# A convolution, routing and expert kernel with its first 32 row tiles in six groups instead of five, a first chunk of 12 tiles, and ranks formed by 0/1 products

## The chip, the cores and the metric

One core of a Trainium2 chip. The metric is device time in microseconds (us) of one execution of the whole program; lower is better. The engines are named PE (matrix products; PEld is its weight load), DVE (vector), ACT (scalar activation), POOL (GpSimd) and SP (which issues most DMAs).

## What is computed

x has 8 sequences of 3584 rows with 192 values. Each of 8 heads (24 columns) gets its own causal convolution of 7 taps, whose taps are a softmax of `weight`. The 28672 resulting rows go through a routed feed-forward layer with 8 experts, where each row goes to its best expert alone.

```python
w = exp(weight - max); w /= sum(w) + 1e-9          # 8 heads x 7 taps
y[b, s, head] = sum_k w[head, k] * x_pad[b, s + k, head]
logits = y @ w_gate + modality_bias[modality_id]   # 28672 x 8
e = argmax(logits); gate = softmax(logits)[e]
out = gate * (relu(y @ w1[e]) @ w2[e])             # 192 -> 1024 -> 192
```

## The kernel before

**Tiles, groups, chunks.** A tile is 120 rows of one sequence; 4 tiles are a quad, and `QUADS_OF_GROUP` cuts the 240 tiles into 18 groups. For each group (class `Group`) the kernel loads x (`load`, L284), convolves it head by head as a product with a band matrix made from the taps (`convolve`, L304: PE into PSUM, ACT or DVE copies it to `y`), turns each quad by a DVE transpose (`turn`, L344), multiplies by the gate weights (`gate`, L362), turns the product back and adds the modality bias (`logits`, L372), picks the expert (`choose`, L382), and ranks the rows (`place`, L416). The rank of a row is its expert's base plus the number of earlier rows of that expert. `send` (L445) then scatters each tile's rows by an indirect DMA on POOL into the DRAM buffer `routed_rows`, sorted by expert. Several groups form a chunk (`GROUPS_OF_CHUNK`).

**Slots.** When a chunk is ranked, `table` (L556) finds which experts have enough rows for a full slot. A slot of the first chunk is 512 rows of one expert, a slot of the second 1024; the first two chunks have two slots each. A slot (class `Slot`) loads the expert's weights (L678 to L683) and its rows (`bring`, L689), splits both in a high and a low part on ACT and DVE (L102, L104), and runs steps: `first` (L775) multiplies rows by 128 columns of w1 (five products of 512 columns, L784), ACT and DVE make the activated `hh` and `hl` (L787, L788), and `second` (L791), two steps later, multiplies those by w2 (L802, L806). `put` and `store` write the result.

**Order.** In the head, `start` (L977) runs the groups of the first chunk to the end, loads the first slot's rows, then runs the groups of the second chunk. From there `run` (L923) goes through the steps and, by the table `marks` of due times, lets the remaining groups advance a piece at a time between steps; `prepare` adds one piece of the next chunk's table per step. Within an engine the program is one fixed order; engines wait for each other by semaphores. On each engine a waiting instruction holds back everything behind it.

**What the change touches in the head.** `WARM` (L26) is the number of products without use that run while the first inputs arrive. The gate weights are laid out in `make_gate` (L175), the band in `make_bands` (L142), the modality ids in `make_modality` (L196), all before the first group. Early groups (`whole_x`, `whole_y`) are convolved and gated in full fp32. Their x tiles share two buffers, `xh` and `xl` (L269), so a later group's x waits until an earlier group is convolved.

```python
w1b = [const.tile([P, 4, FF], F32R, name="w1b0")]                       # L94
self.x = xp.tile([P, NT, D], F32, name="x", tag=self.place_x)           # L269
ins = nc.scalar.dma_start(out=scr[DUMMY:DUMMY + TW, :]...               # L645
```

Of the kernel before, what the change touches and what calls it, by code (L numbers as in the profile page):

```python
# [28 lines left out]
AHEAD = 0  # L29
UNIT = 256  # L30
LONG = 512
GROUPS_OF_CHUNK = (3, 2, 2, 2, 2, 2, 2, 2, 1, 0, 0)
# [9 lines left out]
def conv_then_routed_ffn(ctx, tc, x, weight, modality, w_gate, mod_bias, w1, w2, out):  # L42
# [21 lines left out]
    assert NG == sum(GROUPS_OF_CHUNK) and sum(QUADS_OF_GROUP) == 2 * NSB and NB == 8 and DB == 64 and CAP < 32768 and N % TW == 0  # L64
# [29 lines left out]
    w1b = [const.tile([P, 4, FF], F32R, name="w1b0")]  # L94
    w2b = [const.tile([P, NF, 2 * D], F32R, name="w2b0")]
# [35 lines left out]
    for n in {4 * q for q in QUADS_OF_GROUP}:  # L131
        keep[n] = const.tile([MB, E, n], F32, name=f"keep{n}")
        nc.vector.memset(keep[n], 1.0)
        nc.vector.memset(keep[n][:, :, 0:1], 0.0)
# [5 lines left out]
                   base=0, channel_multiplier=0, allow_small_or_imprecise_dtypes=True)  # L140

    def make_bands():  # L142
# [20 lines left out]
        with tc.issue_after(lined):  # L163
            clear_y()
# [3 lines left out]
        for h in range(0, H, H // 2):  # L168
            nc.sync.dma_start(out=band[:, h:h + H // 2, :], in_=bass.AP(lines.tensor, h * wide, [[1, P], [wide, H // 2], [1, MB]]))
        hi = const.tile([P, H, MB], F32R, name="band_hi")  # L170
        lo = const.tile([P, H, MB], F32R, name="band_lo")
        split(hi, lo, band)
        return band, hi, lo

    def make_gate():  # L175

# [5 lines left out]
        wgs = w1b[0].rearrange("p c n -> p (c n)")[:, 0:NK * 2 * E].rearrange("p (k e) -> p k e", k=NK)  # L182
        nc.scalar.copy(out=wgs[:, :, 0:E], in_=wg)
        nc.vector.tensor_tensor(out=wgs[:, :, E:2 * E], in0=wg, in1=f(wgs[:, :, 0:E]), op=ALU.subtract)
        whole = const.tile([P, NK, P], F32, name="wg_whole", tag="w2b1")
        with tc.issue_after(state["lined"]):
            nc.gpsimd.memset(whole, 0.0)
        parts = const.tile([P, NK, P], F32R, name="wg_parts")
        nc.vector.tensor_copy(out=parts, in_=whole)
        for q in range(P // Q):  # L190
            rows = slice(q * Q, (q + 1) * Q)
            nc.vector.tensor_copy(out=whole[rows, :, q * Q:q * Q + E], in_=wg[rows])
            nc.vector.tensor_copy(out=parts[rows, :, q * Q:q * Q + 2 * E], in_=f(wgs[rows]))
        return whole, parts

    def make_modality():  # L196
# [7 lines left out]
        for half, raw in enumerate(raw2):  # L204
            spare = raw.rearrange("p c d -> p (c d)")
            ids = spare[:, P:P + some * 2 * MB].bitcast(I32).rearrange("p (b u) -> p b u", b=some)
            for i, n in ((0, NSB - 2), (NSB - 2, 2)):
                nc.scalar.dma_start(out=ids[i:i + n],
                                    in_=bass.AP(modality.bitcast(I32).tensor, 2 * (half * some * S + starts[i]),
                                                [[2 * (starts[i + 1] - starts[i]), n], [2 * S, some], [1, 2 * MB]]))  # L210
            low = xp.tile([NSB, some, MB], F32, name="low", tag=f"xr_{half + 1}", bufs=1)
            nc.vector.tensor_copy(out=low, in_=ids[0:NSB].rearrange("p b (s two) -> p b s two", two=2)[:, :, ::-1, 0])
            for b in range(some):
                nc.tensor.transpose(out=mt_ps[:, (half * some + b) * NSB:(half * some + b + 1) * NSB],
                                    in_=low[:, b, :], identity=ident[0:NSB, 0:NSB])
# [16 lines left out]
    def clear_y():  # L232
        for y in y_order:
            nc.gpsimd.memset(y[MB // Q * Q:P], 0.0)
# [12 lines left out]
    def pace(ins):  # L247
        if "result" in state:
            tc.add_manual_dep(ins, state["result"].name,
                              mybir.DependencyInfo(mybir.DependencyClass.Sync, mybir.DependencyReason.DATA), reason="pace")  # L250
# [10 lines left out]
    class Group:  # L261


        def __init__(self, g, chunk):
            self.chunk, self.xr, self.whole_x, self.whole_y = chunk, [], g < WHOLE_X, g < WHOLE_Y
            self.first = g < WHOLE_X
            self.place_x = ("xh", "xl")[g % 2 if self.whole_x else 0]
            if self.whole_x:
                self.x = xp.tile([P, NT, D], F32, name="x", tag=self.place_x)  # L269
            self.quads, before = QUADS_OF_GROUP[g], sum(QUADS_OF_GROUP[:g])  # L270
# [760 lines left out]
```

## Time and profile before

| | us |
|---|---|
| median of 3 runs (1272.39 to 1274.27) | 1272.42 |
| the profiled execution, its own time | 1272.72 |
| its span | 1271.0 |
| PE busy in the span | 1216.2 |
| DVE, ACT, POOL busy | 953.3, 687.3, 538.9 |

The profile page gives busy time per engine over the whole span; it is an average over stages. The span is read in two parts: a head, up to the first product of the first slot (61.10 us, line L784), and the long run of steps behind it. A table of busy time by stretch tells which engine fills a stretch and at which clock PE ran (1.00 is the upper of its two levels, 0.50 the lower). The chain of waits is followed back from the last instruction: it names what was waited for last, in order of time.

### The profile page before, as it was taken

Reading aid. Unit: us, or ns where it says so; the run is one execution under the profiler, and the core shown is the slowest. Engines: PE = TensorE matmul, PEld = TensorE weight load, DVE = VectorE, ACT = ScalarE, POOL = GpSimd, SP = SyncE. Lnnn points to the kernel's source line nnn. Section 1 sums busy time; section 2 is a strip of 40 time slices with the busy share of each in tenths; the row PEclk is TensorE's granted clock in tenths of the full one; section 3 lists DMA queues with packets and bytes.
Section 4 is the critical chain, followed back from the end, with each engine's and each line's share of the span. In section 5 each row is a group of like instructions: output and inputs, shape, how many; then the busy total and the mean of one; then the engine's idle time right before and its main releaser. Section 6 shows DMA issues by size and latency. Waiting matters only on the chain.

```text
span 1271.0 us, 23085 instructions
## 1 busy us (share of the span) xinstructions
PE 1216.2 (96%) x6950; PEld 1085.3 (85%) x6950; DVE 953.3 (75%) x2233; ACT 687.3 (54%) x1486; POOL 538.9 (42%) x549
## 2 busy tenths in 40 slices
PE   8589999999999999999999999999999999999995
PEld 6567777888889898989989888888988888888995
DVE  5767786778788877888778877777775666677894
ACT  3256545555556555555656555555544544555783
POOL 5723673535454534445454634525334322112222
PEclk9899999999999999999999999999999999999998
DMA  5858454442545265522545343524225433696441
GB/s 148 252 138 200 116 166 98 96 121 57 145 96 160 59 145 122 134 47 59 142 95 138 81 113 65 123 57 116 54 58 115 107 58 97 138 248 160 128 110 29
DMA packets 309872, 145.90 MB, mean 115 GB/s; under 512 B 222775, under 2 KB 296160, under 8 KB 309737
## 3 DMA queue, kind: packets, MB, share of 16 engines
q1 hardware_dynamic: 284994, 98.97, 36.2%
q0 software_dynamic: 22464, 44.31, 11.4%
q10 hardware_dynamic: 2279, 1.06, 0.3%
q8 instruction: 56, 0.92, 0.3%
q14 instruction: 79, 0.65, 0.2%
HBM read 114.84 MB, written 51.82 MB: 131 GB/s over the span
## 4 chain that ended last, share of the span: by engine, by line
PE 69%; DVE 12%; issue 6%; DMA 5%; ACT 3%; POOL 3%; SPq 0%; DVEq 0%; POOLq 0%; ACTq 0%
PE hps L784 32%; PE po L802 20%; PE po L806 9%; PE cv L314 4%; PE gt L368 3%; DVE hl L788 2%; POOL out_dram L824 1%; DVE turned L348 1%; DMA routed_rows<-y,idx 1%; DVE sxs L770 1%; DMA raw<-in_moe_w_dram 1%; DVE w1b L104 1%; DVE gx L104 1%; DVE tp L742 1%; DMA rows<-routed_rows 1%
## 5 line engine op out<-in xcount | busy, mean ns | idle before, releaser
L802 PE MATMUL po<-w2b,hh 128*128 128x384 f32 x1824 | 556.9, 359 | 5.5 <-DVE o L820 4.7
L806 PE MATMUL po<-w2b,hl 128*128 128x192 f32 x1824 | 458.9, 252 | 0.0
L787 ACT ACTIVATE hh<-hps 128x512 fp32r<-128x512 f32 x456 | 272.2, 598 | 344.3 <-PE hps L784 330.6
L788 DVE SCALAR_TENSOR_TENSOR hl<-hps,hh 128x512 fp32r<-128x512 f32 x456 | 310.6, 684 | 192.1 <-ACT hh L787 189.3
L824 POOL DMA_INDIRECT out_dram<-o,tags x228 | 244.2, 1071 | 374.3 <-DVE o L820 208.9
L784 PE MATMUL hps<-sxh,w1b 128*128 128x512 f32 (+1 forms) x976 | 385.7, 398 | 9.0 <-DVE hl L788 8.5
L241 POOL DMA_INDIRECT routed_rows<-y,idx x220 | 240.9, 1095 | 318.6 <-DVE hl L788 134.4
L802 PEld LDWEIGHTS po<-w2b,hh 128*128 128x128 f32 x1824 | 343.0, 188 | 31.5 <-DVE o L820 9.6
L806 PEld LDWEIGHTS po<-w2b,hl 128*128 128x128 f32 x1824 | 347.8, 191 | 18.4
L784 PE MATMUL hps<-sxs,w1b 128*128 128x512 f32 (+1 forms) x976 | 291.9, 380 | 0.0
L784 PEld LDWEIGHTS hps<-sxh,w1b 128*128 128x128 f32 x976 | 184.3, 189 | 36.8 <-DVE hl L788 13.8
L784 PEld LDWEIGHTS hps<-sxs,w1b 128*128 128x128 f32 x976 | 179.4, 188 | 38.2
L784 PE MATMUL hps<-sxl,w1b 128*128 128x512 f32 (+1 forms) x488 | 185.6, 380 | 0.0
L104 DVE TENSOR_TENSOR w1b<-raw,w1b 128x512 fp32r<-128x512 f32 x148 | 99.9, 685 | 18.4 <-ACT w1b L102 16.7
L818 ACT ACTIVATE lowp<-po,tags 128x192 f32<-128x192 f32 x228 | 83.8, 420 | 38.0 <-DVE o L820 31.9
L784 PEld LDWEIGHTS hps<-sxl,w1b 128*128 128x128 f32 x488 | 93.2, 191 | 3.6 <-DVE sxl L770 0.2
L102 ACT CAST w1b<-raw 128x512 fp32r<-128x512 f32 x148 | 89.6, 618 | 10.0 <-DMA raw<-in_moe_w_dram 9.3
L820 DVE SCALAR_TENSOR_TENSOR o<-po,tags,lowp 128x192 f32<-128x192 f32 x228 | 83.8, 408 | 14.0 <-ACT lowp L818 13.8
L319 ACT COPY y<-cv 120x192 f32<-120x192 f32 (+1 forms) x192 | 51.7, 320 | 73.7 <-PE cv L314 66.4
L104 DVE TENSOR_TENSOR w2b<-raw,w2b 128x384 fp32r<-128x384 f32 x148 | 79.7, 548 | 14.8 <-ACT w2b L102 14.8
L102 ACT CAST w2b<-raw 128x384 fp32r<-128x384 f32 x148 | 73.7, 511 | 0.7
L768 ACT CAST sxh<-tp 128x512 fp32r<-128x512 f32 (+1 forms) x60 | 35.7, 596 | 49.5 <-DVE tp L742 48.8
(161 smaller groups left out, 975.0 us busy)
## 6 DMA issues: line engine op xcount, KB each, us to landing
raw<-in_moe_w_dram SPq DMA_DIRECT2D x37, 768.0 KB
raw<-in_moe_w_dram SPq DMA_DIRECT2D x37, 512.0 KB
raw<-in_moe_w_dram SPq DMA_DIRECT2D x74, 256.0 KB
rows<-routed_rows SPq DMA_DIRECT2D x208, 64.0 KB
xr<-in_x_dram SPq DMA_DIRECT2D x32, 384.0 KB
x<-in_x_dram SPq DMA_DIRECT2D x26, 384.0 KB
ends<-routed_rows SPq DMA_DIRECT2D x208, 32.0 KB
routed_rows<-filler SPq DMA_DIRECT2D x8, 776.0 KB
```

Source lines behind the costliest of these rows:

```text
L102: nc.scalar.copy(out=hi, in_=raw)
L104: return nc.vector.tensor_tensor(out=lo, in0=raw, in1=f(hi), op=ALU.subtract).ins
L241: state["scatter"] = nc.gpsimd.indirect_dma_start(out=scr, out_offset=bass.IndirectOffsetOnAxis(ap=idx, axis=0), in_=src, in_offset=None,).ins
L319: nc.scalar.copy(out=y[0:MB, 0:self.nb, ys], in_=src)
L784: nc.tensor.matmul(hps[:, u, :], wa[:, c, fs], mv[z], start=n == 0, stop=n == len(terms) - 1)
L787: nc.scalar.activation(out=hh, in_=hps, func=AF.Relu)
L788: state["result"] = nc.vector.scalar_tensor_tensor(out=hl, in0=hps, scalar=0.0, in1=f(hh), op0=ALU.max, op1=ALU.subtract).ins
L802: nc.tensor.matmul(po, hh[:, u, js], wb[:, c, :], start=c == 0, stop=c == NF - 1, skip_group_check=True)
L806: nc.tensor.matmul(po[:, 0:D], hl[:, u, js], wb[:, c, 0:D], start=False, stop=False, skip_group_check=True)
L818: nc.scalar.activation(out=lowp, in_=po[:, D:2 * D], func=AF.Copy, scale=gate)
L820: nc.vector.scalar_tensor_tensor(out=o, in0=po[:, 0:D], scalar=gate, in1=lowp, op0=ALU.mult, op1=ALU.add)
L824: st = nc.gpsimd.indirect_dma_start(out=out, out_offset=bass.IndirectOffsetOnAxis(ap=tag.bitcast(I32)[:, j, 1:2], axis=0), in_=o, in_offse ...
```

## The change

- The first eight quads form six groups (1, 1, 1, 1, 2, 2 quads) instead of five (1, 1, 2, 2, 2). The first chunk has three groups, which are now 12 tiles (16 before); the second has three groups, 20 tiles (16 before). The other groups and all slots stay as they are.
- x of groups 2 to 5 gets buffers of its own (`x_first`, `x_next`) in the space of the first split weights; the loads are issued behind the band's load and wait for no earlier group.
- For these groups the rank is formed in PSUM alone: 0/1 products add the expert's base, all earlier tiles, and the earlier rows of the tile (`place_early`). The scan, the copies of counts and one addition on DVE go.
- The first 8 heads are convolved ahead of the modality ids, the gate layout, the tables and the filler. The gate weights are cleared by DVE and laid out by ACT. What only later groups need (the band's and the gate's split parts) is made just before the first slot (`make_late`). The rows of filler are written behind the first exponential.
- `choose` makes the one-hot choice ahead of the exponential.
- Group 6 (four quads, the first that is not in full fp32 gating) is convolved at the end of the head; `parts_of` counts its heads no longer. The last group of the head is chosen and placed behind that.
- `WARM` falls from 50 to 34.

```diff
-QUADS_OF_GROUP = (1, 1, 2, 2, 2) + (4,) * 13
-WHOLE_X = 10
-WHOLE_Y = 5
+QUADS_OF_GROUP = (1, 1, 1, 1, 2, 2) + (4,) * 13
+WHOLE_X = 11
+WHOLE_Y = 6
-WARM = 50
+WARM = 34
-GROUPS_OF_CHUNK = (3, 2, 2, 2, 2, 2, 2, 2, 1, 0, 0)
+GROUPS_OF_CHUNK = (3, 3, 2, 2, 2, 2, 2, 2, 1, 0, 0)
...
-    w1b = [const.tile([P, 4, FF], F32R, name="w1b0")]
-    w2b = [const.tile([P, NF, 2 * D], F32R, name="w2b0")]
+    x_first = const.tile([P, 16, D], F32, name="x_first", tag="w1b0")
+    x_next = const.tile([P, 8, D], F32, name="x_next", tag="w2b0")
+    w1b, w2b = [], []
...
+    def fill_gate():
         for q in range(P // Q):
             rows = slice(q * Q, (q + 1) * Q)
+            with tc.issue_after(state["ids"]):
+                nc.scalar.copy(out=wg_whole[rows, :, q * Q:q * Q + E], in_=wg[rows])
+
+    def make_late():
...
+        split(hi, lo, band)
...
+        split(wgs[:, :, 0:E], wgs[:, :, E:2 * E], wg)
...
+        nc.scalar.copy(out=parts.rearrange("p k (h n) -> p (k h) n", h=2), in_=filler[:, 2:2 + P // 2].unsqueeze(1).broadcast_to([P, 2 * NK, P // 2]))
...
             else:
-                nc.sync.dma_start(out=xr, in_=x[b0:b0 + 4, starts[sb] - HALO:starts[sb] + MB, :].rearrange("b s d -> s b d"))
+                with tc.issue_after(state["band" if self.g <= WHOLE_Y else "load"]):
+                    nc.sync.dma_start(out=xr, in_=x[b0:b0 + 4, starts[sb] - HALO:starts[sb] + MB, :].rearrange("b s d -> s b d"))
...
+        def place_early(self, after):
+
+            n = self.tiles
+            oh = self.oh
+            rp = self.bank("place", [MB, n + 1, E], F32, "rp")
+            terms = [(rp[:, 0:n, :], tri, oh), (rp[:, n, :], ones, oh[:, n - 1, :]), (rp[:, 1:n, :], ones, oh[:, 0:n - 1, :])]
+            terms += [(rp[:, t:n + 1, :], ones, oh[:, 0:n + 1 - t, :]) for t in range(2, n + 1)]
+            row = tri[0:1, 0:1].broadcast_to([1, E])
+            if self.chunk == 0:
+                terms = [(rp, ones, head_oh[:, t, :].unsqueeze(1).broadcast_to([MB, n + 1, E])) for t in range(self.before)] + terms
+                row = starts_of
+            terms = [(rp, ones[0:1, :], row.unsqueeze(1).broadcast_to([1, n + 1, E])), *terms]
+            for i, (dst, wt, mv) in enumerate(terms):
+                state["ranked", self.g] = nc.tensor.matmul(dst, wt, mv, start=i == 0, stop=i == len(terms) - 1).ins
...
+            if after.g == WHOLE_Y:
+                for h in range(H):
+                    after.convolve(h)
+                    yield
+                state["ready"] = True
+                yield
+            cur.choose()
...
-        through("groups", 1)
...
+        while "ready" not in state:
+            advance()
+        with tc.issue_after(state["exp"]), tc.issue_after(state["placing"]):
+            state["late"] = make_late()
...
         with tc.issue_after(state["placing"]):
             made[i].turn(0)
-        while state["parts"] < head + AHEAD:
-            with tc.issue_after(state["vector"]):
+        with tc.issue_after(state["vector"]):
+            while state["groups"] < FIRST:
                 advance()
```

**PE ahead of the first slot's rows.** `cv` is a convolution, `gt` the gate product, `rp` the rank product, and the `po` rows are the transposes of the first slot's rows; before:

```order
L368 MATMUL gt<-turned,wg_whole 128x128 x9
L314 MATMUL cv<-x,band 120x384 x2
L422 LDWEIGHTS tri
L422 MATMUL rp<-oh,tri 120x64
L423 LDWEIGHTS ones
L423 MATMUL rp<-oh,ones 120x64
L751 MATMUL po<-raw_1_88,raw_1_86 128x128 x4
```

and with the change:

```order
L390 MATMUL gt<-turned,wg_whole 128x128 x4
L336 MATMUL cv<-x,band 120x384
L390 MATMUL gt<-turned,wg_whole 128x128 x6
L336 MATMUL cv<-x,band 120x384 x7
L826 MATMUL po<-raw_1_88,raw_1_86 128x128 x4
```

All eight heads of the first four-quad group (two before) now stand ahead of the transposes.

**POOL's first scatters.** `y...` is the source of a group's scatters; an IOTA ahead of them writes the row numbers; before:

```order
L412 IOTA raw_1_86 120x4
L241 DMA routed_rows<-raw_1_86,idx 238592x194 x4
L412 IOTA y_218 120x4
L241 DMA routed_rows<-y_218,idx 238592x194 x4
L412 IOTA y_219 120x8
L241 DMA routed_rows<-y_219,idx 238592x194 x8
```

and with the change:

```order
L252 DMA routed_rows<-raw_1_86,idx 238592x194 x4
L438 IOTA y_183 120x4
L252 DMA routed_rows<-y_183,idx 238592x194 x4
L438 IOTA y_184 120x4
L252 DMA routed_rows<-y_184,idx 238592x194 x4
```

The first chunk ends with the 12th scatter instead of the 16th.

**DVE between the first two steps of the first slot.** `hl` is a step's second half; with the change:

```order
L422 TENSOR_REDUCE first<-rk 120x8
L433 TENSOR_REDUCE den<-ex 120x8
L423 TENSOR_TENSOR oh<-rk,first 120x64
L434 TENSOR_SCALAR den<-den 120x8
L104 TENSOR_TENSOR w2b_852<-raw_0_87,w2b_852 128x2x192
L436 RECIPROCAL y_185<-den 120x8
L485 TENSOR_TENSOR pos<-rp,carry 120x64
L487 TENSOR_TENSOR carry<-rp,carry 120x8
L486 TENSOR_TENSOR pos<-pos,oh 120x64
```

Before, only the four passes on `w2b` stood there; the last head group's choice and rank now stand among them.

## Rows read from the trace of the kernel before

**Rows 1.** The page: span, and PE's busy time, share and instructions.

```profile
span 1271.0 us, 23085 instructions
PE 1216.2 (96%) x6950; PEld 1085.3 (85%) x6950; DVE 953.3 (75%) x2233; ACT 687.3 (54%) x1486; POOL 538.9 (42%) x549
```

**Rows 2.** Busy time by stretch: stretch, its length, engines, PE clock, DMA share, GB/s.

```profile
50.00:60.00 10.00, 0.86 (x5) 0.78 (x6) 4.08 (x11) 2.28 (x4) 7.85 (x9) 0.68 0.76 202
80.00:90.00 10.00, 8.79 (x49) 7.55 (x48) 9.91 (x24) 7.30 (x15) 0.00 (x0) 1.00 0.00 0
...
200.00:1200.00 1000.00, 990.57 (x5618) 890.55 (x5617) 757.59 (x1680) 553.38 (x1164) 416.24 (x412) 1.00 0.46 107
```

**Rows 3.** The chain of waits, its first 100 us: start, length, what.

```profile
16.97 8.53 DMA x<-in_x_dram
...
50.50 4.83 DMA routed_rows<-y,idx
55.53 3.67 DMA raw<-routed_rows
...
90.32 4.84 DMA raw<-in_moe_w_dram
```

**Rows 4.** Timeline, ACT: start, length, instruction, idle time before it and releaser.

```profile
12.34 0.99 ACT L102 CAST band_hi<-band 128x960 fp32r<-128x960 f32 x1 [4.35 <-DMA band<-tap_lines]
```

**Rows 5.** Timeline, PE's products; a head or gate of fp32 is two instructions.

```profile
14.57 3.60 PE L314 MATMUL cv<-x,band 128*120 128x96 f32 x32
...
20.14 2.94 PE L368 MATMUL gt<-turned,wg_whole 128*128 128x128 f32 x24 [1.97 <-DVE turned L348]
...
34.50 2.11 PE L314 MATMUL cv<-x,band 128*120 128x192 f32 x12
...
59.33 1.09 PE L751 MATMUL po<-raw,raw 128*128 128x128 f32 x4 [9.14 <-DMA raw<-routed_rows]
...
61.10 1.22 PE L784 MATMUL hps<-sxh,w1b 128*128 128x512 f32 x2
...
75.05 1.47 PE L314 MATMUL cv<-x,band 128*120 128x384 f32 x4
```

**Rows 6.** Timeline, PE: the two rank products of one group.

```profile
36.77 0.24 PE L422 MATMUL rp<-oh,tri 120*120 120x64 bf16 x1 [0.16 <-DVE oh L401]
...
36.85 0.22 PE L423 MATMUL rp<-oh,ones 120*120 120x64 bf16 x1
```

**Rows 7.** Timeline, DVE: first and last pass of one choice, and one turn.

```profile
34.70 0.32 DVE L375 STREAM_TRANSPOSE lt<-gt 128x128 f32<-128x128 f32 x1 [0.50 <-PE gt L368]
...
36.51 0.21 DVE L401 TENSOR_TENSOR oh<-rk,first 120x64 bf16<-120x64 f32 x1
...
37.84 0.96 DVE L348 STREAM_TRANSPOSE turned<-y_early 128x768 f32<-128x768 f32 x1
```

**Rows 8.** Timeline, POOL: the first scatter, and two that follow each other.

```profile
30.01 1.18 POOL L241 DMA_INDIRECT routed_rows<-raw,idx  x1 [9.71 <-ACT y L319]
...
32.80 0.99 POOL L241 DMA_INDIRECT routed_rows<-raw,idx  x1 [0.30 <-issue]
34.10 0.99 POOL L241 DMA_INDIRECT routed_rows<-raw,idx  x1 [0.30 <-issue]
```

**Rows 9.** Busy time by stretch around two pauses of PE, columns as in rows 2.

```profile
24.00:25.00 1.00, 0.00 (x0) 0.00 (x0) 0.17 (x2) 0.00 (x0) 0.00 (x0) 1.00 0.64 192
...
27.00:28.00 1.00, 1.00 (x5) 1.00 (x5) 0.91 (x6) 0.32 (x1) 0.00 (x0) 0.50 0.00 1
...
42.00:44.00 2.00, 0.00 (x0) 0.00 (x0) 2.00 (x20) 0.38 (x2) 1.39 (x2) 1.00 0.98 299
```

**Rows 10.** Timeline, the ninth step, and the first product of the twelfth.

```profile
84.46 0.69 DVE L788 SCALAR_TENSOR_TENSOR hl<-hps,hh 128x512 fp32r<-128x512 f32 x1
...
85.21 0.50 PE L784 MATMUL hps<-sxh,w1b 128*128 128x512 f32 x1 [1.13 <-DVE hl L788]
...
99.81 0.68 PE L784 MATMUL hps<-sxh,w1b 128*128 128x512 f32 x1
```

More of the change, by code (lines that the diff above doesn't have):

```diff
@@ L168, in make_bands @@
         for h in range(0, H, H // 2):
[L169 to L173, printed above, removed]
+            state["load"] = nc.sync.dma_start(out=band[:, h:h + H // 2, :], in_=bass.AP(lines.tensor, h * wide, [[1, P], [wide, H // 2], [1, MB]])).ins
+        state["band"] = state["load"]
+        return band
     def make_gate():
@@ L276, in bank @@
         def bank(self, use, *args):
-            if self.chunk < 2 and use == "conv":
+            if self.g <= WHOLE_Y and use == "conv":
                 return ring(ps_g2, 4, *args, "po")
-            if self.chunk < 2 and use == "place":
+            if self.whole_y and (use == "logit" or use == "place" and self.g + 1 < WHOLE_Y):
                 return ring(ps_g1, 2, *args, "hps")
@@ L468, in body @@
         if after:
-            for q in range(min(3, after.quads)):
+            for q in range(after.quads if cur.whole_y else min(3, after.quads)):
                 after.load(q)
-        for h in range(H):
+        for h in range(H if cur.g != WHOLE_Y else 0):
             cur.convolve(h)
@@ L474, in body @@
         cur.bias_of()
+        if cur.whole_y:
+            for q in range(cur.quads):
+                cur.turn(q)
+                yield
+                cur.logits(4 * q, cur.gate(cur.part_turned(q)))
+                yield
+            if after.g == WHOLE_Y:
+                for h in range(H):
+                    after.convolve(h)
+                    yield
+                state["ready"] = True
+                yield
+            cur.choose()
+            yield
+            return
         gates = []
-        ready, step_of = [], 1 if cur.whole_y else 2
+        ready, step_of = [], 2
         for t in range(cur.quads + 2):
@@ L855, in advance @@
         state["parts"] += 1
+    nc.gpsimd.memset(y_first[MB // Q * Q:P], 0.0)
+    band = make_bands()
+    wg, wg_whole = make_gate()
+    for _ in range(H):
+        advance()
+    clear_y(state["lined"])
+    with tc.issue_after(state["lined"]):
+        start_row, step, mt, early_bias = make_modality()
+        fill_gate()
+        init_tables()
+        filler = make_filler()
     def through(what, chunk):
@@ L866, in steps_of, with pace_of_parts @@
         return plan[chunk][2] * NF // LONG
-    head = sum(parts_of(g) for g in range(FIRST)) + WAIT + 1 + QUADS_OF_GROUP[FIRST - 1]
-    marks, steps = [(2, head + AHEAD)], 0
-    for c in range(1, last):
-        steps += plan[c - 1][1] * steps_of(c - 1)
-        g = sum(GROUPS_OF_CHUNK[:c + 1])
-        if not GROUPS_OF_CHUNK[c]:
-            break
-        if c == 1:
-            continue
-        marks.append((steps - LEAD, head + sum(parts_of(i) for i in range(FIRST, min(g + 1, NG)))
-                      + (WAIT + 2 + 4 * QUADS_OF_GROUP[-1] if g == NG else 0)))
+    def pace_of_parts(head):
+        marks, steps = [(2, head)], 0
+        for c in range(1, last):
+            steps += plan[c - 1][1] * steps_of(c - 1)
+            g = sum(GROUPS_OF_CHUNK[:c + 1])
+            if not GROUPS_OF_CHUNK[c]:
+                break
+            if c == 1:
+                continue
+            marks.append((steps - LEAD, head + sum(parts_of(i) for i in range(FIRST, min(g + 1, NG)))
+                          + (WAIT + 2 + 4 * QUADS_OF_GROUP[-1] if g == NG else 0)))
+        return marks
     def due(step):
@@ L998, in conv_then_routed_ffn @@
     start(0)
+    marks = pace_of_parts(state["parts"])
+    band_hi, band_lo, wg_parts = state["late"]
     with tc.manual_schedule(engines=ORDERED):
```

126 lines of the change are left out of this document (78 added, 48 removed).

## The prediction

> **What bounds the kernel now.** First the page: PE is busy 1216.2 of 1271.0 us [rows 1]. That is an average, so I read the table by stretch next: between 200 and 1200 PE works 990.57 of 1000 at clock 1.00 [rows 2]. Behind the head the time is PE's own work, and nothing can be won there but products. In the head it is otherwise: from 50 to 60 PE is busy 0.86 of 10 us [rows 2]. The chain of waits says why. The 16th scatter of the first chunk starts at 50.50 and lands 4.83 later; the load of the first slot's rows starts at 55.53 and takes 3.67 [rows 3]. PE's timeline goes on from there: the transposes of these rows start at 59.33, after 9.14 idle, and the first product of the first slot at 61.10 [rows 5]. Call that product F. It comes 61.10 - 50.50 = 10.6 behind the start of the chunk's last scatter, and 1.77 behind the start of the transposes. The chain also names the transfer of group 2's x, 16.97 to 25.50 [rows 3], during which PE stands still: 0.00 busy from 24 to 25 [rows 9]. So two things in the head are waits: x of group 2, and the last scatter with its load.
>
> The written orders differ in the head and in some 35 steps behind it; the sixteen scatters become twelve, and from there on every slot, its steps and its products are the same. So the sum is: how much earlier is F, and how much of that is kept.
>
> **F with the change, from PE.** The order puts all of this ahead of the transposes: 32 heads of 96 columns for groups 0 to 3, at 3.60 / 16 = 0.225 (32 instructions, two to a head) [rows 5]: 32 x 0.225 = 7.2. Groups 4 and 5 have 16 heads of 192 columns at 2.11 / 6 = 0.35: 5.6. Group 6 has 8 heads of 384 at 1.47 / 2 = 0.74: 5.9. Eight gates at 2.94 / 2 = 1.47: 11.8. Rank products: 52 stand ahead of the transposes (10 in all five groups before); they are at most 72 columns wide, and the nearest row is the pitch from 36.77 to 36.85, 0.08 [rows 6]: 4.2. Sum 34.7.
>
> It starts when the band lands, 12.34 [rows 4]. Before, the first convolution stood at 14.57 [rows 5], behind the gate layout and the longer run of warm products; both are out of the way now, so I take 12.3, with up to 2.2 more as the other bound. Without a wait the transposes would start at 47.0. But each of the six groups goes from PE to DVE and back: a turn (0.96) ahead of each gate, and a choice of 36.72 - 34.70 = 2.0 ahead of the rank products [rows 7]. The order lays another group's convolution under these, so not all shows. Bounds: nothing, and 6 x 2.0 = 12. I take one turn per group, 5.8, since the convolutions beside it (1.8 for a one-quad group) cover a choice nearly, not a choice and a turn. Transposes at 52.8, F at 52.8 + 1.77 = **54.6**, with bounds 48.8 and 60.8. That is 6.5 ahead of 61.10.
>
> **Is it the scatters instead?** Group 0: convolved by 14.1, group 1's convolution behind it till 15.9, gate to 17.4, choice to 19.4, as much again for place and row numbers: the first scatter at about 22, against 30.01 [rows 8]. The pitch is 34.10 - 32.80 = 1.30 [rows 8], so the twelfth starts at about 22 + 11 x 1.30 = 36, or later by what group 2 waits for PE. Plus 10.6: 47. The rows are there before PE is through, by this sum; what is late next is PE's row of convolutions and gates, with DVE's turns between.
>
> **What hides the rest.** x of groups 1 to 6 is eleven quads of 128 x 4 x 192 values of 4 bytes, 4.3 MB; at the 192 GB/s of 24 to 25 [rows 9] that takes 22 us and is done some 32 us into the span, a quad every 2.0 us in the order in which PE asks for them, 1.8 us of convolution and 1.47 of gate apart. Group 1's x now stands behind the band on SP's queue; a quad's 2.0 behind 12.34 is 14.3, where PE is done with group 0 at 14.1, so nothing is lost. The filler write goes behind the first exponential, where only scatters use the DMAs. The late split parts (a 0.99 cast of the band [rows 4], a like one for the gate) lie on ACT and DVE under group 6's convolution on PE; if that cover is gone they cost up to 3. POOL clears six `y` tails ahead of the scatters, while it waits anyway (9.71 idle before the first scatter [rows 8]). The shorter rank (no scan) takes DVE work from a chain that I count in the choices. These I put at nothing.
>
> **Behind F.** Before, DVE is full from 80 to 90 (9.91 of 10 [rows 2]): the ninth step's products at 85.21 wait 1.13 for `hl`, which starts at 84.46 [rows 10]. Then the third slot's weights are fetched at 90.32 and take 4.84 [rows 3], and the twelfth step's first product is at 99.81 [rows 10], that is F + 38.7. So the 6 heads of group 6 that go ahead of the transposes (6 x 0.74 = 4.4) leave a stretch in which PE waits for DVE; I count nothing for them there, and F + 38.7 stays. DVE gets the choice and rank of the last head group between the first two steps' halves: about two choices' worth, 0 to 4 on the third step, into a DVE that is full. Behind the twelfth step PE is the bound, and what PE has done by then counts fully: by the orders the change has one gate (1.47) and one head (0.74) fewer left, 2.2.
>
> **The sum.** 6.5 + 2.2 = 8.7. The profiled execution took 1272.72, 0.30 above the median of 1272.42; 1272.7 - 8.7 = **1264.0**. A measurement of this kernel tells some 0.2%, 2.5 us, from no change.
>
> A rule that speaks against this change stands beside a row. From 24 to 25 PE was idle, and from 27 to 28, fully busy again, it had clock 0.50; yet after nothing at all from 42 to 44 that stretch still shows 1.00 [rows 9]. The Trainium skill, "TensorE: Matmul & The Clock Gate", section "What's actually happening", says that the engine is held at the lower clock unless its recent activity keeps it released. The first pause agrees with that rule, the second does not within its own stretch. This is rival C below.
>
> The same page's section "Wait — 56ns, not 53.3ns?" puts the start-to-start floor of small products at about 25 ns. By that the 52 rank products would be an estimated 1.3, and the time about 1261; rows 6 show 0.08, and the sum goes by that.
>
> **The rivals.**
> A. *DVE does not bind behind F, or the head's turns are hidden.* Then the 4.4 of group 6's six heads count too: 1264.0 - 4.4 = 1259.6; with F at 48.8 instead it is 1258.2. For it: PE still does 8.79 in 80 to 90 [rows 2], so less work there could shorten something. Against: 9.91 of DVE in the same row. 0.20.
> B. *Every group shows a whole choice.* F at 60.8, gain 0.3 + 2.2 = 2.5: 1270.2. For it: with one-quad groups there is little to lay under a choice. Against: the convolutions are ordered ahead of the gates they would wait for. 0.12.
> C. *Slower: PE is granted 0.50 through much of the head.* There are 16 fewer warm products and six small groups with a pause each. Every us of PE's 34.7 that runs at half clock costs one more. It decides from 8.7 + 2.5 = 11.2 us of work at 0.50; with 20 of the 34.7, F is at 74.6 and the time 1284. For it: the 0.50 from 27 to 28. Against: 1.00 through 42 to 44, with PE idle [rows 9], and pauses here of about 1. 0.07.
> D. *The first chunk of 12 tiles does not fill two slots, and work without rows runs instead.* The routing of the given inputs puts 727 and 683 rows of this chunk on its two fullest experts, over the 512 of a slot, so the change does what it says. 0.01.
> The forecast keeps 0.60.
>
> **How the numbers follow.** The likeliest case with its own unknowns (F by 3 either way) spans 1261 to 1267. The range takes in A (down to 1258.2, and a little more if the start moves too) and nearly all of B: 1257.5 to 1270.5; C, D and B's edge are left out. Faster by over 0.2%: forecast and A, 0.80. Within: B, 0.12. Slower: C and D, 0.08.
>
> **What would show it.** In the profile after: band landing near 12, first scatter near 22, no idle PE for x of group 2, the twelfth scatter near 36 and the rows landed before PE is through with group 6; F near 54.6 with PE, not a DMA, released by DVE's turns just before; the twelfth step near F + 38.7, still behind the weights' 4.84. I am wrong if the transposes wait for the rows again (then the scatters are the limit), if clock 0.50 shows over more than 10 us of the head, if F to the twelfth step is shorter by 4 (A) or longer by 4 (DVE's extra choice), or if PE's busy time behind 200 differs.

## The result, and the profile after

The change takes 1261.21 us (median of 4 runs, 1260.41 to 1262.08) against 1272.87 beside it: a ratio of 0.9907, interval 0.9890 to 0.9924. That is 11.7 us less; the forecast was 8.7 less, 1264.0 in a range of 1257.5 to 1270.5. The profiled execution took 1261.50, its span is 1259.8 (1271.0 before).

The page after, span and PE; PE's work is the same within 0.4 us [rows 1], so what was won is waiting:

```profile
span 1259.8 us, 23209 instructions
PE 1215.8 (97%) x7002; PEld 1084.7 (86%) x7002; DVE 948.5 (75%) x2215; ACT 691.7 (55%) x1507; POOL 538.7 (43%) x549
```

Busy time by stretch after, columns as in [rows 2]. The stretch from 50 to 60, where PE did 0.86, now holds 8.63. Behind 200 nothing changed (990.07 for 990.57). The low place that the kernel before has at 90 to 100 (the first line here, 5.64) stands at 80 to 90 in the change (4.91), with clock 0.75 behind it.

```profile
90.00:100.00 10.00, 5.64 (x29) 4.63 (x28) 7.23 (x17) 4.05 (x9) 1.01 (x1) 0.90 0.90 237
...
40.00:50.00 10.00, 8.58 (x48) 6.90 (x48) 8.03 (x28) 7.13 (x20) 6.42 (x8) 0.83 0.78 221
50.00:60.00 10.00, 8.63 (x43) 5.57 (x42) 6.94 (x21) 7.04 (x22) 6.00 (x7) 1.00 0.77 202
80.00:90.00 10.00, 4.91 (x30) 4.13 (x30) 5.14 (x18) 1.74 (x4) 1.05 (x2) 0.91 0.76 182
90.00:100.00 10.00, 10.00 (x40) 8.07 (x41) 7.05 (x23) 5.41 (x15) 3.10 (x3) 0.75 1.05 254
200.00:1200.00 1000.00, 990.07 (x5652) 890.00 (x5651) 762.65 (x1693) 556.33 (x1167) 413.36 (x407) 1.00 0.47 108
```

PE's timeline after: start of the convolutions, the small rank products of one group and what follows them, one of the three turn waits, the transposes of the first slot's rows, F, the wait for the third slot's weights, and the twelfth step's first product.

```profile
11.95 2.13 PE L336 MATMUL cv<-x,band 128*120 128x96 f32 x16 [0.80 <-DMA band<-tap_lines]
...
21.16 0.42 PE L479 MATMUL rp<-head_oh,ones 120*120 120x8 bf16 x5
21.43 0.47 PE L390 MATMUL gt<-turned,wg_whole 128*128 128x128 f32 x2
...
42.51 0.71 PE L390 MATMUL gt<-turned,wg_whole 128*128 128x128 f32 x4 [1.42 <-DVE turned L370]
...
52.72 0.60 PE L826 MATMUL po<-raw,raw 128*128 128x128 f32 x4
...
54.00 0.73 PE L859 MATMUL hps<-sxh,w1b 128*128 128x512 f32 x2 [0.25 <-ACT sxh L843]
...
89.99 0.69 PE L877 MATMUL po<-w2b,hh 128*128 128x384 f32 x1 [5.09 <-DVE o L895]
...
92.98 1.20 PE L859 MATMUL hps<-sxh,w1b 128*128 128x512 f32 x1
```

The last wait names DVE, but DVE waited for ACT, and ACT for the transfer of the third slot's weights:

```profile
86.14 0.62 ACT L102 CAST w1b<-raw 128x512 fp32r<-128x512 f32 x1 [6.89 <-DMA raw<-in_moe_w_dram]
```

F is at 54.00 (61.10 before [rows 5]), 7.1 earlier. The transposes show no idle time before them: PE, not the rows, was last. PE's busy time from the first convolution to the transposes:

```profile
12.00:52.70 40.70, 35.44 (x266) 31.15 (x267) 25.71 (x124) 21.52 (x81) 25.72 (x35) 0.96 0.79 222
```

On POOL and SP the first scatter, the twelfth, and the issue of the rows' load:

```profile
23.56 1.19 POOL L252 DMA_INDIRECT routed_rows<-raw,idx  x1 [5.49 <-ACT y L341]
...
38.41 0.99 POOL L252 DMA_INDIRECT routed_rows<-y,idx  x1 [0.30 <-DVE idx L496]
```

```profile
45.04 0.39 SPq L788 DMA_DIRECT2D raw<-routed_rows  x1
```

**Where the 11 us of span came from.** The step's second half `hl` on DVE marks one step of 456. The lead over the kernel before is read at the 12th, 40th, 441st and last; first before, then after:

```profile
102.86 0.68 DVE L788 SCALAR_TENSOR_TENSOR hl<-hps,hh 128x512 fp32r<-128x512 f32 x1
...
199.34 0.68 DVE L788 SCALAR_TENSOR_TENSOR hl<-hps,hh 128x512 fp32r<-128x512 f32 x1
...
1220.12 0.68 DVE L788 SCALAR_TENSOR_TENSOR hl<-hps,hh 128x512 fp32r<-128x512 f32 x1
...
1256.40 0.69 DVE L788 SCALAR_TENSOR_TENSOR hl<-hps,hh 128x512 fp32r<-128x512 f32 x1 [1.64 <-ACT hh L787]
```

```profile
96.24 0.69 DVE L863 SCALAR_TENSOR_TENSOR hl<-hps,hh 128x512 fp32r<-128x512 f32 x1 [0.60 <-ACT hh L862]
...
185.62 0.68 DVE L863 SCALAR_TENSOR_TENSOR hl<-hps,hh 128x512 fp32r<-128x512 f32 x1
...
1206.48 0.68 DVE L863 SCALAR_TENSOR_TENSOR hl<-hps,hh 128x512 fp32r<-128x512 f32 x1
...
1245.45 0.69 DVE L863 SCALAR_TENSOR_TENSOR hl<-hps,hh 128x512 fp32r<-128x512 f32 x1 [1.64 <-ACT hh L862]
```

The lead is 7.1 at F, 6.6 at the 12th step, 13.7 at the 40th, 13.6 at the 441st and 10.95 at the last. So the forecast's two terms (6.5 and 2.2) were exceeded by the 40th step, and some 2.7 were lost again in the last passes. The table by stretch, from the 12th to the 40th step, before and after:

```profile
102.86:199.34 96.48, 89.00 (x473) 73.52 (x471) 74.47 (x191) 49.12 (x117) 53.42 (x57) 1.00 0.58 144
```

```profile
96.24:185.62 89.38, 85.63 (x461) 71.72 (x459) 71.59 (x177) 48.98 (x114) 51.33 (x54) 1.00 0.56 137
```

Of the 7.1 won there, 89.00 - 85.63 = 3.4 are PE work that is not left to do, and the other 3.7 are less idle time (7.48 before, 3.75 after). Which work it is, the same stretches show for the gate (`gt`) and the convolutions (`cv`) alone; the first share is PE's, with the number of products. Before, gate and convolution, then after:

```profile
102.86:199.34 96.48, 9.04 (x60) 7.57 (x60) 2.23 (x5) 1.00 0.58 144
102.86:199.34 96.48, 15.48 (x40) 6.25 (x40) 0.00 (x0) 10.28 (x38) 1.00 0.58 144
```

```profile
96.24:185.62 89.38, 7.32 (x48) 6.16 (x48) 1.72 (x4) 1.00 0.56 137
96.24:185.62 89.38, 14.66 (x38) 5.90 (x38) 0.00 (x0) 9.86 (x36) 1.00 0.56 137
```

That is a gate of 12 products and one head less. In the tail the last pass's first product waits 2.35, where it was 1.05, and then PE runs at clock 0.66. PE's timeline and the stretch behind it after, then PE's timeline before:

```profile
1234.78 0.39 PE L859 MATMUL hps<-sxh,w1b 128*128 128x256 f32 x1 [2.35 <-DVE hl L863]
```

```profile
1235.00:1240.00 5.00, 5.00 (x29) 5.00 (x29) 2.88 (x6) 0.60 (x1) 1.03 (x1) 0.66 0.06 21
```

```profile
1247.29 0.39 PE L784 MATMUL hps<-sxh,w1b 128*128 128x256 f32 x1 [1.05 <-DVE hl L788]
```

### The profile page after: what moved, and what is told of

Same layout as the page of the kernel before. It is cut to its first block, busy times and chain, and to the rows that moved or that the text cites. A ratio compares the mean times of both kernels' runs of the same rounds, so it can differ in the third digit from the quotient of the medians.

```text
span 1259.8 us, 23209 instructions
## 1 busy us (share of the span) xinstructions
PE 1215.8 (97%) x7002; PEld 1084.7 (86%) x7002; DVE 948.5 (75%) x2215; ACT 691.7 (55%) x1507; POOL 538.7 (43%) x549
## 5 line engine op out<-in xcount | busy, mean ns | idle before, releaser
L252 POOL DMA_INDIRECT routed_rows<-y,idx x224 | 247.7, 1106 | 317.5 <-DVE hl L863 140.5
L895 DVE SCALAR_TENSOR_TENSOR o<-po,tags,lowp 128x192 f32<-128x192 f32 x228 | 83.8, 408 | 13.6 <-ACT lowp L893 13.6
```

The lines of the kernel that those rows point to most:

```text
L252: state["scatter"] = nc.gpsimd.indirect_dma_start(out=scr, out_offset=bass.IndirectOffsetOnAxis(ap=idx, axis=0), in_=src, in_offset=None,).ins
L895: nc.vector.scalar_tensor_tensor(out=o, in0=po[:, 0:D], scalar=gate, in1=lowp, op0=ALU.mult, op1=ALU.add)
```

## The experiments

These ran later than the first measurement, on four chips of the same kind that the record numbers 0 (again, g6_behind, warm50, table2), 8 (chunk16, x_shared, scan, before_p), 2 (again_b, conv_early, both) and 1 (filler_early). The number of the chip of the first measurement is not on record; it is called the first chip below. On the four, the kernel before takes 1288.1 to 1289.5 us by the median, some 16 more than on the first. Each ratio is to the kernel before on the same chip; F and steps come from one profile each.

| run | what is edited in the change | median us | ratio | interval |
|---|---|---|---|---|
| again | nothing | 1271.50 | 0.9874 | 0.9853 to 0.9894 |
| again_b | nothing | 1269.95 | 0.9860 | 0.9838 to 0.9883 |
| g6_behind | group 6's heads behind the transposes | 1276.91 | 0.9910 | 0.9894 to 0.9927 |
| warm50 | 50 warm products | 1270.22 | 0.9859 | 0.9842 to 0.9876 |
| table2 | second table in 3 pieces a step | 1266.96 | 0.9836 | 0.9805 to 0.9867 |
| chunk16 | first chunk of 16 tiles | 1279.43 | 0.9918 | 0.9898 to 0.9939 |
| x_shared | x of groups 2 to 5 in the old buffers | 1278.69 | 0.9923 | 0.9905 to 0.9942 |
| scan | rank by scan | 1273.11 | 0.9879 | 0.9860 to 0.9897 |
| filler_early | filler written early | 1274.28 | 0.9877 | 0.9851 to 0.9903 |
| conv_early | convolutions may go one rank earlier | 1274.11 | 0.9901 | 0.9881 to 0.9921 |
| both | table2 and conv_early | 1267.84 | 0.9843 | 0.9821 to 0.9865 |
| before_p | the kernel before | 1290.83 | 1.0007 | 0.9995 to 1.0019 |

**again, again_b.** No edit.

> The changed kernel, unchanged, for a second profile. Open is the tail: in the first profile the lead over the kernel before is 13.8 us at the 40th step, is still 13.8 at the 440th, and is 11.0 at the last, since PE waits 2.35 us (1.05 before) ahead of the last pass and then runs 1235 to 1240 at clock 0.66. Theory N (the transfers of the last passes vary from run to run): this wait comes out anywhere between about 0.8 and 2.5, and the time of the whole follows it. Theory S (the change shifts the phase of the last passes against their loads): 2.3 again, with the lower clock behind it. The time by both is 1259.5 to 1262.

> The change, unchanged, as the measure for the two runs beside it and for the place of its pauses. Expected as on the same chip: 1270 to 1275, F 60 to 61, a pause of 4 to 5 near 30 to 32 and the lower clock behind it; by theory N of the tail, the wait ahead of the last pass is anywhere from 0.3 to 2.4.

Neither theory's time came: on these chips the same program behaves otherwise in the head, and otherwise from profile to profile. F came at 60.70 and, where 60 to 61 was expected again, at 55.77. In the first, PE pauses 4.49 ahead of group 3's gate, and the next ten us have clock 0.66; in the second the pause is 1.40 and the clock of that stretch 1.00. The timeline of `again`, all engines, and the stretch:

```profile
26.10 1.53 PE L390 MATMUL gt<-turned,wg_whole 128*128 128x128 f32 x12
...
27.46 0.56 PE L336 MATMUL cv<-x_first,band 128*120 128x96 f32 x4
...
29.76 0.32 DVE L397 STREAM_TRANSPOSE lt<-gt 128x128 f32<-128x128 f32 x1 [4.57 <-remote]
...
31.21 0.24 ACT L341 COPY y_early<-cv 120x96 f32<-120x96 f32 x1 [1.17 <-remote]
...
32.52 2.08 PE L390 MATMUL gt<-turned,wg_whole 128*128 128x128 f32 x8 [4.49 <-DVE turned L370]
```

```profile
30.00:40.00 10.00, 7.48 (x42) 7.03 (x43) 6.65 (x54) 2.60 (x11) 5.11 (x7) 0.66 0.17 47
```

DVE and ACT wait for products whose records end at 27.63 (gate) and 28.02 (convolution); they go on at 29.76 and 31.21, and the trace names nothing that held them ("remote"). So a single F is good to some 5 us here, and below a verdict rests on the medians and on a wait that is seen. The wait ahead of the last pass was 2.35, 1.27 and 1.62 in three profiles of this one program (0.76 to 2.37 in the other runs, under 0.6 in warm50 and scan): theory N. Nothing here shows that the change causes the 2.35, so the loss in the tail is put to no step of it.

**g6_behind.**

```diff
             if after.g == WHOLE_Y:
+                state["ready"] = True
+                yield
                 for h in range(H):
                     after.convolve(h)
                     yield
-                state["ready"] = True
-                yield
...
-        with tc.issue_after(state["placing"]):
+        with tc.issue_after(state["placing"]), tc.issue_after(state["gate"]):
             made[i].turn(0)
```

> Seven of group 6's eight heads stand behind the transposes of the first slot's rows instead of ahead of them; nothing else is changed. The rows' load is issued at 45.0 and, as before, should be there some 4 later, 3 to 3.5 ahead of the transposes at 52.7. Theory P (PE's work is what counts in the steps, so a head that is done ahead of the first product is gained in full): F falls by 2 to 3.5, but the 7 x 0.74 = 5.2 come back in the steps; at the 40th step this kernel is 2 to 3 behind the change, and it is slower by 1.5 to 3. Rival D (the forecast's: DVE binds behind F and the moved heads are worth nothing there): the steps keep their distance from F, so it is faster by 2 to 3.5. If the rows are not there earlier, F stays within 0.7 and it is slower by 4 to 5 (P) or the same (D).

F came at 57.06, 3.6 ahead of `again`, but the 12th step is 4.3 behind it and the 40th 4.5. From the transposes to the end of the second step's products it takes 10.1 us (53.17 to 63.26), where `again` takes 4.3 (59.42 to 63.75). The seven heads are 5.2 of these 5.8, so up to there they count in full, as theory P has it. What follows is a new wait, and the clock behind it. DVE goes on at 64.98, though the records of the rank products that it waits for end at 61.54; then PE, and the stretch:

```profile
64.98 0.22 DVE L485 TENSOR_TENSOR pos<-rp,carry 120x64 f32<-120x64 f32 x1 [4.79 <-remote]
```

```profile
67.17 0.79 PE L859 MATMUL hps<-sxh,w1b 128*128 128x512 f32 x1 [3.91 <-DVE hl L863]
```

```profile
60.00:70.00 10.00, 6.09 (x28) 4.50 (x27) 5.12 (x16) 4.19 (x12) 4.96 (x5) 0.77 0.85 220
```

The median is 5.4 above `again`. Rival D of these runs (not the prediction's D: the reading that DVE hides moved work, on which the forecast's zero rested) asked for a faster kernel and falls for the first two steps. But the 5.4 are not the price of the heads alone: the late release is of the kind told of in the last section, and up to it this kernel was 0.5 ahead. And the kernel before had these heads in later steps (from 68.42 to 79, the third to the seventh step); what they cost there was not tried.

**warm50.**

```diff
-WARM = 34
+WARM = 50
```

> The 16 products without use are put back (50 instead of 34), nothing else. They take 9.76 / 34 = 0.29 each, 4.6 in all, and PE's last one would end at 15.5 instead of 10.9, where the band lands at 11.9. Theory P: the first convolution starts at 15.5, 3.6 late; the pauses of PE in the head (about 6 in all) may take up to 2 of it, so F and the end are 1.5 to 3.6 later. Rival C (the clock needs the longer run of products): the clock between 12 and 50, 1.00 up to 40 and 0.83 from 40 to 50 with the change, is 1.00 throughout, and the time is the same or lower.

The convolutions began at 13.81 instead of 11.18 in `again`, yet F (60.43) and the time are those of `again`. Neither theory's number came: the 2.6 went into the pauses, and the clock was not 1.00 throughout (0.78 from 30 to 40, where `again` has 0.66). The shorter run of warm products is worth nothing measurable, either way.

**table2.**

```diff
-                    next(prepared.setdefault(chunk + 1, prepare(chunk + 1)), None)
+                    for _ in range(3 if chunk == 0 else 1):
+                        next(prepared.setdefault(chunk + 1, prepare(chunk + 1)), None)
```

> The second chunk's table is made in three pieces a step instead of one. In the change, ACT waits 6.89 at 79 to 86 for the third slot's weights, which are issued at 81.46, a us behind the table's last pieces on DVE (80.4); PE is idle 5.09 ahead of 89.99 and then has clock 0.75 from 90 to 100, which costs 2.5 more. Theory P: the table ends near 67, the weights are issued by 70 and are there at 75, the wait goes, and so does the low clock: faster by 4 to 7. Rival D: DVE, full from 60 to 80, is what PE waits for, and the pieces only move its work: faster by 0 to 1.5. Rival Q (the transfers of the third slot's weights then collide with the last scatters of the second chunk on the queues): the weights land where they did, no gain.

The third slot's weights are issued at 76.12 instead of 88.22, and the stretch in which they were waited for changes; SP's own timeline and the stretch 90 to 100, of `again`, then of table2:

```profile
88.22 0.37 SPq L753 DMA_DIRECT2D raw<-in_moe_w_dram  x1
```

```profile
90.00:100.00 10.00, 5.71 (x20) 4.42 (x20) 6.69 (x22) 4.06 (x10) 3.18 (x4) 0.76 0.97 271
```

```profile
76.12 0.37 SPq L753 DMA_DIRECT2D raw<-in_moe_w_dram  x1
```

```profile
90.00:100.00 10.00, 9.69 (x48) 7.31 (x47) 8.40 (x26) 5.79 (x15) 3.00 (x3) 1.00 0.83 224
```

The wait of 4 to 5 and the low clock are gone, and the median is 4.5 lower than `again` on the same chip, as theory P had it, at its lower end. Its runs spread more (1260.23 to 1274.34), so its interval overlaps a little with those of the two runs of the change. DVE was full here (9.77 from 80 to 90) and it did not matter: rival D falls a second time. The twelfth step's first product stands 93.08 - 58.66 = 34.4 behind F, where `again` has 38.2 and the change on the first chip 39.0:

```profile
93.08 0.69 PE L859 MATMUL hps<-sxh,w1b 128*128 128x512 f32 x1
```

**chunk16.**

```diff
-GROUPS_OF_CHUNK = (3, 3, 2, 2, 2, 2, 2, 2, 1, 0, 0)
+GROUPS_OF_CHUNK = (4, 2, 2, 2, 2, 2, 2, 2, 1, 0, 0)
```

> The first chunk has four groups (16 tiles, as before) and the second two; all the rest of the change stays. The 16th scatter of the first profile starts at 43.79; with 10.6 behind it F is 54.4, where PE itself came to 54.0. Theory P (PE's row sets F): F later by 0.5 to 2 than with 12 tiles, the time by 0 to 2. Rival S (the scatters set F, four fewer of 1.30 are the gain): F later by 4 to 5.2, and the time with it. The ratio to the kernel before would be 0.988 to 0.992 by P and 0.991 to 0.995 by S.

The 16th scatter starts at 50.1 and the rows' load is issued at 56.90; SP, then PE:

```profile
56.90 0.39 SPq L788 DMA_DIRECT2D raw<-routed_rows  x1
```

```profile
35.81 1.43 PE L390 MATMUL gt<-turned,wg_whole 128*128 128x128 f32 x5 [6.27 <-DVE turned L370]
...
66.07 0.60 PE L826 MATMUL po<-raw,raw 128*128 128x128 f32 x4
```

By the load's 3.67 of before the rows are there near 61, 5 ahead of the transposes, which have no wait. So in this profile, in which PE itself was late, not even 16 scatters set F: rival S's mechanism is not there. But the time is 8 above `again`, which P did not allow. F is 67.35; the unexplained pause took 6.27 in this profile, the slowest of the six runs (1285.38), and PE had clock 0.58 and 0.73 from 30 to 50. Behind F another 3.41 of idle time follows ahead of 73.77, with clock 0.66 from 70 to 80. Why it is slower by more than the pause of a run stays open.

**x_shared.** No group takes its x from `x_first` or `x_next`.

```diff
-            if 2 <= g < WHOLE_Y:
+            if g < 0:
```

> x of groups 2 to 5 shares the two buffers of the later groups again, so each load waits for the convolution two groups ahead; the rest of the change stays. A quad takes about 2 us and its latency, so group 2's x can be there at 17 to 18, where PE asks at 21.7; group 3's at 21 to 22 (24.0), group 4's at 27 (32.0), group 5's at 34 (35.3), group 6's four quads, behind group 4's convolution, at 43 to 44 (45.2). Theory G (it is the smaller groups that took the wait away, since their x is one quad): F within 1 of the change's. Rival X (the buffers of their own did it): F later by 4 or more, with PE idle for x of a group.

F is 66.97, and PE waits for a transfer again:

```profile
57.75 1.60 PE L336 MATMUL cv<-x,band 128*120 128x384 f32 x2 [7.37 <-DMA x<-in_x_dram]
```

Groups 2 to 5 show no wait for x, as theory G had it; it is the x of group 6 that comes late, because its loads stand behind the first slot's weights and rows on SP (the last three are issued from 47.92). The price, 7.2 above `again`, is that of rival X. What the buffers of their own bring is that group 6's four quads can be fetched before the weights.

**scan.** Groups 0 to 4 take the old rank; its masks lie in a ninth tile of `x_next`.

```diff
-    x_next = const.tile([P, 8, D], F32, name="x_next", tag="w2b0")
+    x_next = const.tile([P, 9, D], F32, name="x_next", tag="w2b0")
...
+    for n, at in ((4, 0), (8, 4 * E)):
+        keep[n] = x_next[0:MB, 8, at:at + n * E].rearrange("p (e t) -> p e t", e=E)
...
-            if self.whole_y:
+            if self.g + 1 == WHOLE_Y:
                 return self.place_early(after)
```

> The rank of groups 0 to 4 is formed as before, by two products, two copies and a scan on DVE (group 5 stays with the 0/1 products). PE has some 34 small products less, 1.4 to 2.7 us; DVE gets four instructions more of 0.16 to 0.24 for each of five groups, 4 in all, a part of it between the choice and the scatters. Theory P: PE's row sets F, so F is 0 to 2 earlier, or the same since the pauses stay. Rival K (the chain of choice and rank sets the pace, so DVE's four more count each time): F later by 2 to 4. Either way the scatters start up to 1 later each and F does not wait for them.

F at 59.54, 1.2 ahead of `again`; 1273.11, ratio 0.9879, the same as the change. Theory P: for groups 0 to 4 the ranks by 0/1 products bring nothing that can be measured. (The order of PE's products in the head changes with this edit, and with that of filler_early.)

**filler_early.**

```diff
     def lay_filler():
-        with tc.issue_after(state["first_exp"]):
+        with tc.issue_after(state["lined"]):
...
         filler = make_filler()
+        lay_filler()
...
             through("groups", 0)
-            lay_filler()
```

> The filler's 776 KB are written behind the taps (near 11 us), ahead of most of the x loads, as in the kernel before, and not behind the first exponential (20 us); the rest of the change stays. Two things are asked. First, what the later place is worth: 776 KB at the 326 GB/s of the x loads are 2.4 us, so x of groups 2 to 6 comes 2.4 later; it is there 3 or more ahead of PE in the change, so F is the same within 1 (cover holds) or up to 2.4 later (it doesn't). Second, the pause of PE near 28 to 39 on this chip, in which the products' semaphores come 2 to 7 us behind the records of the products, and which follows the filler's transfer: if the filler's transfer brings it, the pause goes, with the lower clock behind it, and F is 3 to 5 earlier; if it is something else, it stays, in size 1.4 to 7.

The time is the same (0.9877). The pause does not go; PE shows it later, and at its longest:

```profile
42.88 1.43 PE L390 MATMUL gt<-turned,wg_whole 128*128 128x128 f32 x5 [8.02 <-DVE turned L370]
```

So the filler's transfer ahead of it does not cause it. Whether x's cover held could not be told apart beside a pause of this size.

**conv_early and both.** `both` has table2's edit too.

```diff
-            with tc.issue_after(state["ranked", self.g - 2]) if 2 <= self.g <= WHOLE_Y else nullcontext():
+            with tc.issue_after(state["ranked", self.g - 3]) if 3 <= self.g <= WHOLE_Y else nullcontext():
```

> A group's convolution may stand ahead of the rank of the group two before it (it waits for that of the group three before); by the written order PE then has group 4's, 5's and 6's heads at hand where it waited for a turn. On the chip of the calls before, the change's pauses in the head were 1.42, 4.49, 0.65, 0.88 and 1.42 us, and clock 0.50 stood for 10.2 us behind them. Theory C2 (the pauses cost themselves and bring the low clock): at least two of the three turn waits go, less than 5 us of 0.50 are left in the head, F is 3 to 7 earlier, and since the rows are there 9 ahead of the transposes, all of that is kept: faster by 3 to 7. Rival W (the waits for the turns only move behind the work that was brought forward): pauses and F stay within 1.

> The second chunk's table in three pieces a step, and the convolutions brought forward, together. The table alone was faster by 4.5 on the median and took the wait of 5.09 for the third slot's weights away. If the two are apart (F by the one, the tenth step by the other), the gains add: 7 to 11 below the change, a ratio to the kernel before of 0.979 to 0.982. Rival: with an earlier F, DVE's steps meet the last scatters and the table again, and the sum is no better than the table alone (0.9836).

The turn waits did go from PE's list, and one pause took their place, with nothing named; `both`, PE:

```profile
39.33 0.99 PE L336 MATMUL cv<-x_next,band 128*120 128x192 f32 x2 [7.65 <-issue]
```

F is 61.27 and 60.69, no earlier than `again`, and conv_early is 4.2 slower than `again_b` on the same chip (0.9901, 0.9860). C2 falls, and W describes it better: from 12 us to F, PE is idle 12.4 and 12.0, where `again` has 10.1 and `again_b` 7.7. `both` (0.9843) is no better than table2 alone, so the gains do not add. But it is 6.3 faster than conv_early on the same chip, with intervals that do not meet: a second and clearer sign of what the table in three pieces brings. The best version found is table2, by 4.5 us on the median below the change on that chip; it was not run on the first chip.

**before_p.**

> The kernel before, unchanged, for a profile on the chip of the runs below. In the call before this one it took 1289 us, against 1272 at first, while the change took 1271.5 against 1261; PE stood idle 4.49 us ahead of 32.52 there (1.34 at first) with inputs that were late by PE's own end of the products ahead, and had clock 0.50 for 6.8 us behind it. Theory C2 (a pause of several us in the head is what brings clock 0.50, and on this chip the pauses are longer): the profile shows F later than 61.10 by several us, more than 0.50 in the head and the steps, and a step time behind 200 that is the same. Rival M (this chip's memory is slower throughout): the time between the 46th and the 440th step, 1003 at first, is longer by 5 or more.

F is at 67.86, 6.8 later than on the first chip, with clock 0.67, 0.54 and 0.66 in the three stretches from 50 to 80, as theory C2 expected; that the pauses bring the low clock is not shown by it. From the 46th step to the 441st it takes 1237.54 - 231.14 = 1006.4, where it took 1004.5: rival M asked for 5 or more and falls. What the chip takes lies ahead of the 46th step (6.8 by F, 8.8 more from there, 231.14 for 215.59), and 2.5 in the tail; the kernel before loses more to it than the change, so the ratio is lower there.

## Why the prediction was right, and where it was not

- *The start at the band's landing, near 12:* it is 11.95. That the shorter warm-up does not matter, warm50 shows. The x loads behind it came at 281 and 298 GB/s (10 to 20 and 20 to 30 us), not at the 192 of the prediction's sum, so there was more cover than it counted.
- *PE's row ahead of the transposes, 34.7 of work and 5.8 of waits, transposes at 52.8:* they began at 52.72; from 12.00 to 52.70 PE was busy 35.44 and idle 5.26. F is 54.00 for 54.6. Inside the sums terms were off and nearly met, which is luck: the rank products stand 0.27 / 5 = 0.054 apart, not 0.08, so 52 of them are 2.8 and not 4.2; and from 40 to 50 the clock was 0.83, which costs about 1.7. The idle time is not one turn of 0.96 for each of six groups: it is three waits for a turn (1.41, 1.34, 1.42) and some short ones, one of 0.59 for the x of group 1, which the prediction put at nothing. The Trainium skill's floor for small products ("TensorE: Matmul & The Clock Gate", "Wait — 56ns, not 53.3ns?") would have given an estimated 1.3; these, each with a weight load of its own, were measured at about twice its 25 ns.
- *The scatters are not the limit:* the first came at 23.56 (22), the twelfth at 38.41 (36), and the transposes waited for PE alone. In chunk16's profile 16 were not the limit either; on the first chip that would have been close, by the 54.4 worked out above for 16 scatters against an F of 54.0. Of the change's parts, the x buffers (x_shared) carry a measurable price, and group 6's place (g6_behind) one whose size is not settled; ranks, warm-up and the filler's place carry none; the 12 tiles' part is not settled. The six groups, the earlier choice and the late split parts were not run apart.
- *F to the twelfth step stays:* 38.7 was forecast and 92.98 - 54.00 = 39.0 came. The zero for the six moved heads is right as a number, but the runs point to another reason than a full DVE. The twelfth step is held by the third slot's weights: PE is idle 5.09 ahead of 89.99, with the low clock behind it. table2, where this wait is gone and DVE is as full, has the step 34.4 behind F, 3.8 less than `again`. So rival A, for which F to the twelfth step had to be shorter by 4, did not come about; that the 3.8 are the moved heads is argued, not shown. In the heads' place PE does a gate more on that way (24 products of the gate up to the 12th `hl`, 13 before; 2 of convolutions, 12 before), and this is the gate that is not left to do later.
- *The term that was too small:* "Behind the twelfth step PE is the bound", and with it "2.2". The lead grew by 7.1 between the 12th and the 40th step, 4.9 more than the 2.2. The work was told rightly, one gate and one head less; it came to 3.4 of PE's busy time. But PE is not the bound there: it was idle 7.48 of 96.48 before and 3.75 of 89.38 after, and this 3.7 is what the sum lacks. Why it fell is open. On the other chips the changed program is idle for 7.16 (`again`) and 6.23 (`again_b`) in this stretch, so the change alone does not bring it.
- *What hid this:* 2.7 lost in the last passes, of which the prediction says nothing. By the three profiles of one program the wait there varies from profile to profile. The time came near the forecast partly by luck, since 4.9 too little and 2.7 too much stand against each other.
- *Rival C:* it asked for the low clock through the head. On the first chip it shows in 40 to 50 alone (0.83, behind the wait of 1.42), on the other chips over more (0.66 from 30 to 40 in `again`); it decided nowhere, since the kernel before has it too there. Its rule in the Trainium skill ("TensorE: Matmul & The Clock Gate", "What's actually happening") agrees with each of these stretches: the lower level follows a pause, and full work brings 1.00 back. Not every pause shows it: behind the 1.40 in `again_b` the stretch has 1.00. B did not come about: the idle time came to 5.26 in all, not 12.

## What to carry to other kernels

Fill the wait with work that must be done anyhow, and then look for the next wait behind it. The heads that were moved into the wait for the scatters did not shorten the way from F to the twelfth step (38.7 before, 39.0 after): PE waited for the third slot's weights on it. A busy share did not tell this: DVE was at 9.91 of 10 us there, and as full in table2, where the wait was gone. These weights hung on a table made one piece a step, and three pieces a step took the wait away. When a wait is filled, ask again what the other parts of the change still buy; with 12 tiles PE, and no scatter, was last ahead of the first slot. And where a sum says that an engine is the bound, read its idle time in that stretch first: PE had 7.48 us of it between the 12th and the 40th step.

## What was not expected of the hardware

On the later chips, in most profiles, PE's products in the head release their readers late: in `again` 2.1 us behind the end of the gate's records (27.63, 29.76) and 3.2 behind the last convolution's (28.02, 31.21), with no transfer or engine named, and in other builds the same shows as a pause of 6 to 8 us (6.27, 7.65, 8.02) between 30 and 43. It moved with the program's order, varied between two profiles of one program on two chips (4.49 and 1.40) and stayed when the filler's transfer was taken away from ahead of it. In g6_behind the same shows behind F (61.54, 64.98). Its cause is open; with the low clock behind it, it is most of what makes F vary by 5 us there.
